# A pooled-attention and softmax-linear feed-forward kernel: first product from pairs of float16 numbers, scaled by powers of two, and one square moved to ScalarE

## The chip, the core and the metric

One Trainium2 chip, one core of it. The time is device time of the launch in microseconds (us). The core's engines are TensorE (PE in the rows, with its weight loads as PEld), VectorE (DVE), ScalarE (ACT), GpSimd (POOL) and SyncE (SP, which here only issues transfers). Each engine takes its instructions in program order and waits on semaphores of the others.

## What is computed

Attention over keys pooled 4x4, followed by a feed-forward block whose middle is h times softmax(h), normalised. The input tensors are float32, apart from w_in and w_out, whose scaling makes them float64.

```python
# attention, per batch of 4: 12288 queries, 768 pooled keys, C = 128
kv_flat = kv.reshape(B, H//4, 4, W//4, 4, C).mean(axis=(2, 4)).reshape(B, -1, C) @ w_sr
k = v = kv_flat
a = softmax((q @ k.T) / sqrt(C))
x = (a @ v).reshape(B * 12288, 128)
# feed-forward, d_ff = 1024
h = x @ w_in                      # the "first product" of the title
e = exp(h - h.max(-1)); sm = e / e.sum(-1)
solu = h * sm
ln = (solu - solu.mean(-1)) / sqrt(solu.var(-1) + 1e-6) * g_ln
out = ln @ w_out
```

## The kernel before, in words

Tokens go in 384 tiles of 128 (4 batches of 96 tiles); four tiles are a group (96 groups). A tile passes a chain of steps, and a loop over 399 slots takes one step of each of several tiles per slot: in slot t the scores of tile t (and the matmuls of tile t+1), and ten slots later (LH) the hidden layer of that tile, thirteen slots later (LO) its last product. From slot 9 (FILL) to six slots past the last tile the order written in the loop is the order on every engine (`manual_schedule`); before and after, a scheduler orders the work.

Precision comes from pairs: a number is a high part plus a low part, and a product is three matmuls (high with high, high with low, low with high). The scores (`scores_pe`, L359) and the first product (`hidden_pe`, L455) use pairs in a float32 format that the PE takes in one pass (f32r; the page of the profile shows it as f32). The other two, attention times values (`values`, L412) and the last product (`final_pe`, L540), use pairs of float16. Per tile that is 6 matmuls of 384 columns, 4.5 of 512 (18 for each group), 6 of 512 and 24 of 128.

What a group of four tiles does once, at slots counted within the group:

- `values_out` on ACT: two scaled copies of the attention output out of PSUM, the high part `xh` (L421) and a full float32 copy `xf` (L422).
- `values_split` on POOL: the low part `xl = xf - xh` (L428). `values_norm` on POOL: `zz` (L435).
- `final_scale` on POOL: four instructions on 4 columns, `f = (z2 + 1e-9) * bound` (L553), `f2 = f * f` (L556), plus `v3` (L557), and the power -1/2 (L558). In the POOL queue they stand ahead of the splits of that slot.
- `q_split` on ACT (L337) and `q_low` on POOL (L345), `rz` on DVE and ACT (L440, L441), the output `ob` on DVE (L564).

What each tile does on POOL: `hidden_split`, the high part of u (L507) and the low part (L508). On ACT: the exponent of the scores (L376), its scaled copy (L378), the square with a sum for the variance (L521), the exponent of h (L476). On DVE: maximum of the scores (L375), u (L490), maximum of h (L461) and its product with 1/z (L467), the low half of the probabilities (L386).

For the next batch, `PLAN` gives slots of the running batch: loads, then 30 additions on POOL (`kv_add`, L201, every second slot from 9 to 67), and from slot 41 on the steps that make keys, values, the norm (`kv_norm_pe`, `kv_norm_out`, `kv_norm_max`) and the bound (`kv_bound`, DVE and POOL, parts at slots 103 and 104, that is 7 and 8 of the batch that uses it). The first batch does the same in `kv_now` and `fill`. The last batch makes nothing for a next one.

At the start w_in is turned from float64 words into a float32 part `wf` and a rest `wr` (`float64_parts`), ACT makes `w_in_h` (L617) and the squares (L619), the PE and DVE the largest column norm `wmax2` (L624), and POOL makes `w_in_l` (L642, L645).

Of the kernel before, what the change touches and what calls it, by code (L numbers as in the profile page):

```python
# [21 lines left out]
P = 128  # L22
# [30 lines left out]
def kernel(  # L53
# [32 lines left out]
    def pow2_under(dst):  # L86

        nc.vector.tensor_single_scalar(
            dst.bitcast(I32), dst.bitcast(I32), 0x7F800000, op=ALU.bitwise_and
        )  # L90
# [33 lines left out]
    def kv_alloc(b):  # L124
        for n, w, dt, bufs in (
            ("kT", NK, F32, 1),
            ("ks", NK, F32, 1),
            ("kh", NK, F32R, 2),
            ("kl", NK, F32R, 2),
            ("ksq", NK, BF16, 1),  # L130
            ("kss", 2, F32, 1),
            ("knm", 2, F32, 1),
            ("vf", NK, F32, 1),
            ("sv", 2, F32, 2),
            ("bb", 2, F32, 2),
        ):
            state[n, b] = bat.tile([P, w], dt, tag=n, name=f"{n}_{b}", bufs=bufs)
        for n in ("vh", "vl"):
            state[n, b] = bat.tile([P, NKC, P], F16, tag=n, name=f"{n}_{b}")
# [125 lines left out]
    def kv_bound(b, part):  # L265

        knm, bb = state["knm", b], state["bb", b]
        if part == 0:
            nc.vector.tensor_tensor(bb[:, 0:1], knm[:, 0:1], knm[:, 1:2], op=ALU.max)
            nc.vector.tensor_scalar(  # L270
                bb[:, 0:1], bb[:, 0:1], wmax2, 1e-20, op0=ALU.mult, op1=ALU.max
            )
            nc.gpsimd.tensor_tensor(bb[:, 0:1], bb[:, 0:1], mhalf[:, 0:1], op=ALU.pow)
        else:
            nc.vector.tensor_scalar(
                bb[:, 1:2], bb[:, 0:1], SC * 1e-3 * 2.0**15, None, op0=ALU.mult
            )
            nc.vector.tensor_scalar(bb[:, 0:1], bb[:, 0:1], SC, None, op0=ALU.mult)

    def kv_vs(b, half):  # L280
# [135 lines left out]
    def values_out(g):  # L416
        b = g * GT // TPB
        xa, sv = state.pop(("xa", g)), state["sv", b][:, 1:2]
        xf = grp.tile([P, 512], F32, tag="xf", name=f"xf_{g}", bufs=1)
        xh = grp.tile([P, 512], F32R, tag="xh", name=f"xh_{g}")  # L420
        nc.scalar.activation(xh, xa, AF.Copy, scale=sv)  # L421
        nc.scalar.activation(xf, xa, AF.Copy, scale=sv)  # L422
        state["xf", g] = (xf, xh)

    def values_split(g):
        xf, xh = state.pop(("xf", g))
        xl = grp.tile([P, 512], F32R, tag="xl", name=f"xl_{g}")
        nc.gpsimd.tensor_tensor(xl, xf, xh.bitcast(F32), op=ALU.subtract)  # L428
        state["x", g] = (xh, xl)

    def values_norm(g):
        b = g * GT // TPB
        zz = grp.tile([P, GT], F32, tag="zz", name=f"zz_{g}", bufs=2)
        rz = grp.tile([P, 2, GT], F32, tag="rz", name=f"rz_{g}", bufs=3)
        nc.gpsimd.tensor_scalar(zz, state.pop(("z", g)), 1e-9, 1.0, op0=ALU.add, op1=ALU.mult)  # L435
        state["zz", g] = (zz, rz)
# [111 lines left out]
    def final_scale(g):  # L548
# [3 lines left out]
        f2 = grp.tile([P, GT], F32, tag="f2", name=f"f2_{g}")  # L552
        nc.gpsimd.tensor_scalar(  # L553
            f, state.pop(("z2", g)), 1e-9, state["bb", b][:, 1:2], op0=ALU.add, op1=ALU.mult
        )
        nc.gpsimd.tensor_tensor(f2, f, f, op=ALU.mult)  # L556
        nc.gpsimd.tensor_tensor(f, f2, state.pop(("v3", g)), op=ALU.add)  # L557
# [27 lines left out]
    w_sr16 = const.tile([P, P], F32, name="w_sr16")  # L585
    w_in_h = const.tile([P, DFF], F32R, name="w_in_h")
    w_in_l = const.tile([P, DFF], F32R, name="w_in_l")
    wch = const.tile([P, NFC, P], F16, name="wch")
    wcl = const.tile([P, NFC, P], F16, name="wcl")
    sw = const.tile([P, 1], F32, name="sw")  # L590
    swi = const.tile([P, 1], F32, name="swi")
    wmax2 = const.tile([P, 1], F32, name="wmax2")

    wsr = const.tile([P, P], F32, name="wsr")
# [21 lines left out]
    wf, wr = float64_parts(raw_in, "in")  # L616
    nc.scalar.copy(w_in_h, wf)  # L617
    wsq = wrk.tile([P, DFF], BF16, tag="junk", name="wsq", bufs=1)
    nc.scalar.activation(wsq, wf, AF.Square)  # L619
    pn = ps_r.tile([P, DFF], F32, tag="r", name="pn")  # L620
    for half in range(2):
        hs = slice(half * 512, half * 512 + 512)
        nc.tensor.matmul(pn[:, hs], ones16, wsq[:, hs], start=True, stop=True)
    nc.vector.tensor_reduce(wmax2, pn, axis=AX.X, op=ALU.max)  # L624

    def kv_now(b, *fs):
# [14 lines left out]
    def w_in_rest():  # L641
        nc.gpsimd.tensor_tensor(wf, wf, w_in_h.bitcast(F32), op=ALU.subtract)  # L642

# [45 lines left out]
    def kv_norms(half):  # L689
# [11 lines left out]
        7: [w_square, partial(kv_bound, 0, 0)],  # L701
        8: [w_norm, partial(kv_bound, 0, 1)],
        9: [w_pow],
# [14 lines left out]
        (77, 0, kv_scale_v), (78, 1, kv_scale_v), (79, 2, kv_scale_v),  # L718
        (79, 0, kv_vs), (81, 1, kv_vs),
        (85, 0, kv_v_pe, kv_norm_out), (87, 0, kv_v_high), (88, 0, kv_v_low),  # L720
        (89, 1, kv_v_pe, kv_norm_out), (91, 1, kv_v_high), (92, 1, kv_v_low),
        (93, 0, kv_norm_pe, kv_norm_out), (96, 0, kv_norm_max),
        (97, 1, kv_norm_pe, kv_norm_out), (99, 1, kv_norm_max),
        (103, 0, kv_bound), (104, 1, kv_bound),
    ]
# [107 lines left out]
```

## Time and profile before

| | us |
|---|---|
| median of three runs | 1951.87 (1951.87 to 1959.1) |
| the profiled execution, its own time | 1954.76 |
| its span, first to last instruction | 1953.0 |
| PE busy, weight loads busy | 1899.8 (97%), 1487.8 (76%) |
| DVE, ACT, POOL busy | 1797.4 (92%), 1783.9 (91%), 1760.0 (90%) |
| granted PE clock, mean | 0.995 of full speed |

All four engines are busy nine tenths of the span or more, so shares of the span don't say which of them sets the pace. A matmul's end in the trace is modelled, and consecutive ones overlap in it: what a matmul costs is read from the distance between starts. Gaps under 0.15 us are an engine's own and are not shown as idle, so POOL's real load is read from its starts as well.

### The profile page before, as it was taken

Reading aid. Unit: us, or ns where it says so; the run is one execution under the profiler, and the core shown is the slowest. Engines: PE = TensorE matmul, PEld = TensorE weight load, DVE = VectorE, ACT = ScalarE, POOL = GpSimd, SP = SyncE. Lnnn points to the kernel's source line nnn. Section 1 sums busy time; section 2 is a strip of 40 time slices with the busy share of each in tenths; the row PEclk is TensorE's granted clock in tenths of the full one; section 3 lists DMA queues with packets and bytes.
Section 4 is the critical chain, followed back from the end, with each engine's and each line's share of the span. In section 5 each row is a group of like instructions: output and inputs, shape, how many; then the busy total and the mean of one; then the engine's idle time right before and its main releaser. Section 6 shows DMA issues by size and latency. Waiting matters only on the chain. (4 is left out here: it accounts for less than half of the span.)

```text
span 1953.0 us, 43521 instructions
## 1 busy us (share of the span) xinstructions
PE 1899.8 (97%) x15678; PEld 1487.8 (76%) x15678; DVE 1797.4 (92%) x2573; ACT 1783.9 (91%) x3141; POOL 1760.0 (90%) x1579
## 2 busy tenths in 40 slices
PE   7999999999999999999999999999999999999997
PEld 4677777777777777777777777777777887787775
DVE  7899999999999999999999999899999999999985
ACT  3998999999999999999999999999999999999995
POOL 3699999999899999999989999999988898988886
PEclk8999999999999999999999999999999999999998
DMA  6899999999999999999999999999999999999996
GB/s 237 174 237 233 235 225 238 221 221 217 213 242 231 238 228 226 226 223 222 217 221 237 237 235 229 228 229 219 223 210 215 223 218 221 225 215 219 224 198 135
DMA packets 1484311, 432.88 MB, mean 222 GB/s; under 512 B 1405889, under 2 KB 1471553, under 8 KB 1483841
## 3 DMA queue, kind: packets, MB, share of 16 engines
q1 hardware_dynamic: 1469840, 410.10, 104.6%
q10 hardware_dynamic: 14256, 20.00, 3.9%
q8 instruction: 125, 2.05, 0.5%
q14 instruction: 90, 0.73, 0.1%
HBM read 52.50 MB, written 25.17 MB: 40 GB/s over the span
## 5 line engine op out<-in xcount | busy, mean ns | idle before, releaser
L508 POOL TENSOR_TENSOR uhl<-u,uhl 128x1024 f16<-128x1024 f32 x384 | 823.2, 2144 | 37.4 <-ACT uhl L505 6.0
L540 PEld LDWEIGHTS <-uT 128*128 128x128 f16 x9216 | 517.5, 98 | 112.8 <-issue 104.6
L540 PE MATMUL o<-wch,uT 128*128 128x128 f16 x6144 | 582.9, 220 | 7.2 <-DMA uT<-uhl 6.8
L540 PE MATMUL o<-wcl,uT 128*128 128x128 f16 x3072 | 536.0, 219 | 0.0
L490 DVE SCALAR_TENSOR_TENSOR u<-h,rz,e 128x1024 f32<-128x1024 f32 x384 | 490.2, 1277 | 24.9 <-ACT e L476 24.5
L461 DVE TENSOR_REDUCE nm<-h 128x1 f32<-128x1024 f32 x384 | 468.9, 1221 | 19.0 <-PE h L455 11.7
L476 ACT ACTIVATE e<-h,nm,rz 128x1024 f32<-128x1024 f32 x384 | 460.1, 1198 | 3.6 <-DVE rz L440 2.8
L521 ACT ACTIVATE junk<-u,su 128x1024 bf16<-128x1024 f32 x384 | 438.0, 1141 | 1.9 <-DVE u L490 1.9
L507 POOL TENSOR_SCALAR uhl<-u 128x1024 f16<-128x1024 f32 x378 | 395.9, 1047 | 10.4 <-DVE u L490 10.2
L412 PE MATMUL xa<-pT,vh 128*128 128x512 f16 x1152 | 391.5, 382 | 7.4 <-DMA pT<-phl 5.2
L375 DVE TENSOR_REDUCE nm<-s 128x1 f32<-128x768 f32 x384 | 365.3, 951 | 34.6 <-PE s L359 34.0
L376 ACT ACTIVATE s<-s,nm 128x768 f32<-128x768 f32 x384 | 335.7, 874 | 60.9 <-DVE nm L375 60.0
L386 DVE SCALAR_TENSOR_TENSOR phl<-s,phl 128x768 f16<-128x768 f32 x384 | 364.9, 951 | 20.0 <-ACT phl L378 10.5
L378 ACT ACTIVATE phl<-s 128x768 f16<-128x768 f32 x384 | 311.4, 811 | 12.0
L455 PE MATMUL h<-w_in_h,xh 128*128 128x512 f32 x768 | 304.9, 478 | 7.0 <-DVE phl L386 3.2
L359 PE MATMUL s<-kh,qh 128*128 128x384 f32 x768 | 264.4, 425 | 7.2 <-DVE u L490 2.8
L455 PE MATMUL h<-w_in_h,xl 128*128 128x512 f32 x768 | 245.1, 400 | 12.0 <-POOL xl L428 11.6
L455 PE MATMUL h<-w_in_l,xh 128*128 128x512 f32 x768 | 240.3, 394 | 0.0
L412 PE MATMUL xa<-pT,vl 128*128 128x512 f16 x576 | 219.1, 380 | 0.0
L359 PE MATMUL s<-kh,ql 128*128 128x384 f32 x768 | 196.2, 337 | 0.0
L359 PE MATMUL s<-kl,qh 128*128 128x384 f32 x768 | 196.1, 336 | 0.0
L455 PEld LDWEIGHTS h<-w_in_h,xh 128*128 128x128 f32 x768 | 140.4, 190 | 72.6 <-issue 18.2
(119 smaller groups left out, 2223.0 us busy)
## 6 DMA issues: line engine op xcount, KB each, us to landing
qf<-in_q_dram SPq DMA_DIRECT2D x96, 256.0 KB, 3.3
out_dram<-ob SPq DMA_DIRECT2D x96, 256.0 KB, 2.8
kv<-in_kv_dram ACTq DMA_DIRECT2D x96, 192.0 KB, 3.1
kv<-in_kv_dram SPq DMA_DIRECT2D x16, 384.0 KB, 7.8
pT<-phl SPq DMA_TRANSPOSE x384, 4.0
uT<-uhl SPq DMA_TRANSPOSE x384, 4.3
raw_in<-in_moe_w_in_dram ACTq DMA_DIRECT2D x1, 1024.0 KB, 6.5
raw_out<-in_moe_w_out_dram SPq DMA_DIRECT2D x1, 1024.0 KB, 7.6
```

The lines of the kernel that those rows point to most:

```text
L359: nc.tensor.matmul(s[:, half, :384], lh[:, ts], rh[:, half * 384 : (half + 1) * 384], start=n == 0, stop=n == 2,)
L375: nc.vector.tensor_reduce(nm, s, axis=AX.XY, op=ALU.max, negate=True)
L386: nc.vector.scalar_tensor_tensor(phl[:, 1], state.pop(("s", t)), SC, phl[:, 0], op0=ALU.mult, op1=ALU.subtract)
L412: nc.tensor.matmul(xa, v[:, c, :], pT[:, :, a * NKC + c, :], start=n == 0, stop=n == len(seq) - 1)
L455: nc.tensor.matmul(h[:, hs], lh[:, ts], rh[:, hs], start=n == 0, stop=n == 2)
L461: nc.vector.tensor_reduce(nm[:, 0:1], state["h", t], axis=AX.X, op=ALU.max, negate=True)
L476: nc.scalar.activation(e, state["h", t], AF.Exp, bias=nm[:, 1:2], scale=state["rz", g][0][:, js], accum_out=state["z2", g][:, js],)
L490: nc.vector.scalar_tensor_tensor(u, state.pop(("h", t)), state["rz", g][1][:, j : j + 1], state.pop(("e", t)), op0=ALU.mult, op1=ALU.mult, ...
L507: nc.gpsimd.tensor_scalar(uhl[:, 0, :], u, 1.0, 1.0, op0=ALU.mult, op1=ALU.mult)
L508: nc.gpsimd.tensor_tensor(uhl[:, 1, :], u, uhl[:, 0, :], op=ALU.subtract)
L521: nc.scalar.activation(junk, u, AF.Square, scale=-float(DFF), bias=su, accum_out=state["v3", g][:, j : j + 1],)
L540: nc.tensor.matmul(po[:, ts], uT[:, a * NFC + c, :], w[:, c, :], start=c == 0 and n == 0, stop=c == NFC - 1 and n == 2,)
```

## The change

x and w_in are split into pairs of float16 in place of f32r, for which both are first scaled by powers of two: w_in by `wsc`, from its largest column norm, and x by a factor from the largest key norm that is multiplied into the scale `sv` of `values_out`. The product of both factors, `bb[:, 3:4]`, is divided out again in `values_norm`, whose second factor was the constant 1.0. The two ACT copies and POOL's subtraction in `values_out` and `values_split` stay and write float16.

In `final_scale` the first two POOL instructions become one ACT instruction, Square with scale and bias from two columns. The loop's order puts it on ACT behind the scaled copy of the scores (L378) and ahead of the square of u (L521) of the same slot.

`kv_bound` gets three parts, at slots 88 to 90 of the batch before, and the norm's steps move ahead of the values' steps, from slots 93 to 99 to slots 77 to 84. At the start, `w_in_h` waits for the norm, and two scalings of 128x1024 are added on ACT.

```diff
-            ("bb", 2, F32, 2),
+            ("bb", 4, F32, 2),
...
+        knm, bb, sv = state["knm", b], state["bb", b], state["sv", b]
         if part == 0:
-            nc.vector.tensor_tensor(bb[:, 0:1], knm[:, 0:1], knm[:, 1:2], op=ALU.max)
+            nc.vector.tensor_tensor(knm[:, 0:1], knm[:, 0:1], knm[:, 1:2], op=ALU.max)
             nc.vector.tensor_scalar(
-                bb[:, 0:1], bb[:, 0:1], wmax2, 1e-20, op0=ALU.mult, op1=ALU.max
+                bb[:, 0:1], knm[:, 0:1], wmax2, 1e-20, op0=ALU.mult, op1=ALU.max
             )
+            nc.vector.tensor_scalar(knm[:, 0:1], knm[:, 0:1], 1e-28, None, op0=ALU.max)
             nc.gpsimd.tensor_tensor(bb[:, 0:1], bb[:, 0:1], mhalf[:, 0:1], op=ALU.pow)
-        else:
+            nc.gpsimd.tensor_tensor(knm[:, 0:1], knm[:, 0:1], mhalf[:, 0:1], op=ALU.pow)
+        elif part == 1:
             nc.vector.tensor_scalar(
                 bb[:, 1:2], bb[:, 0:1], SC * 1e-3 * 2.0**15, None, op0=ALU.mult
             )
             nc.vector.tensor_scalar(bb[:, 0:1], bb[:, 0:1], SC, None, op0=ALU.mult)
+            nc.vector.tensor_scalar(bb[:, 2:3], bb[:, 1:2], 1e-9, None, op0=ALU.mult)
+            pow2_under(knm[:, 0:1])
+        else:
+            nc.vector.tensor_scalar(knm[:, 0:1], knm[:, 0:1], 2.0**5, None, op0=ALU.mult)
+            nc.vector.tensor_scalar(bb[:, 3:4], knm[:, 0:1], wsc, None, op0=ALU.mult)
+            nc.vector.tensor_scalar(sv[:, 1:2], sv[:, 1:2], knm[:, 0:1], None, op0=ALU.mult)
...
-        xh = grp.tile([P, 512], F32R, tag="xh", name=f"xh_{g}")
+        xh = grp.tile([P, 512], F16, tag="xh", name=f"xh_{g}")
...
-        xl = grp.tile([P, 512], F32R, tag="xl", name=f"xl_{g}")
-        nc.gpsimd.tensor_tensor(xl, xf, xh.bitcast(F32), op=ALU.subtract)
+        xl = grp.tile([P, 512], F16, tag="xl", name=f"xl_{g}")
+        nc.gpsimd.tensor_tensor(xl, xf, xh, op=ALU.subtract)
...
-        nc.gpsimd.tensor_scalar(zz, state.pop(("z", g)), 1e-9, 1.0, op0=ALU.add, op1=ALU.mult)
+        nc.gpsimd.tensor_scalar(
+            zz, state.pop(("z", g)), 1e-9, state["bb", b][:, 3:4], op0=ALU.add, op1=ALU.mult
+        )
...
-        nc.gpsimd.tensor_scalar(
-            f, state.pop(("z2", g)), 1e-9, state["bb", b][:, 1:2], op0=ALU.add, op1=ALU.mult
-        )
-        nc.gpsimd.tensor_tensor(f2, f, f, op=ALU.mult)
+        bb = state["bb", b]
+        nc.scalar.activation(
+            f2, state.pop(("z2", g)), AF.Square, scale=bb[:, 1:2], bias=bb[:, 2:3]
+        )
         nc.gpsimd.tensor_tensor(f, f2, state.pop(("v3", g)), op=ALU.add)
...
-    w_in_h = const.tile([P, DFF], F32R, name="w_in_h")
-    w_in_l = const.tile([P, DFF], F32R, name="w_in_l")
+    w_in_h = const.tile([P, DFF], F16, name="w_in_h")
+    w_in_l = const.tile([P, DFF], F16, name="w_in_l")
...
     wf, wr = float64_parts(raw_in, "in")
-    nc.scalar.copy(w_in_h, wf)
...
     nc.vector.tensor_reduce(wmax2, pn, axis=AX.X, op=ALU.max)
+    nc.vector.tensor_scalar(wsc, wmax2, 1e-28, None, op0=ALU.max)
+    nc.gpsimd.tensor_tensor(wsc, wsc, mhalf[:, 0:1], op=ALU.pow)
+    pow2_under(wsc)
+    nc.vector.tensor_scalar(wsc, wsc, 2.0**14, None, op0=ALU.mult)
+    nc.scalar.mul(wf, wf, wsc)
+    nc.scalar.copy(w_in_h, wf)
+    nc.scalar.mul(wr, wr, wsc)
...
-        8: [w_norm, partial(kv_bound, 0, 1)],
+        8: [w_norm, partial(kv_bound, 0, 1), partial(kv_bound, 0, 2)],
...
+        (77, 0, kv_norm_pe, kv_norm_out), (80, 0, kv_norm_max),
+        (81, 1, kv_norm_pe, kv_norm_out), (84, 1, kv_norm_max),
         (85, 0, kv_v_pe, kv_norm_out), (87, 0, kv_v_high), (88, 0, kv_v_low),
+        (88, 0, kv_bound), (89, 1, kv_bound), (90, 2, kv_bound),
         (89, 1, kv_v_pe, kv_norm_out), (91, 1, kv_v_high), (92, 1, kv_v_low),
-        (93, 0, kv_norm_pe, kv_norm_out), (96, 0, kv_norm_max),
-        (97, 1, kv_norm_pe, kv_norm_out), (99, 1, kv_norm_max),
-        (103, 0, kv_bound), (104, 1, kv_bound),
```

## Rows read from the trace of the kernel before

**Rows 1.** busy by stretch: length, then busy of PE, PEld, DVE, ACT, POOL

```profile
131.00:350.00 219.00, 213.17 (x1784) 167.66 (x1784) 201.55 (x287) 202.05 (x357) 209.73 (x188) 1.00 1.15 232
...
1297.00:1893.00 596.00, 593.22 (x4993) 470.21 (x4992) 565.17 (x813) 563.57 (x995) 534.24 (x474) 1.00 1.10 218
```

**Rows 2.** busy time by stretch, of line L376 alone: two instructions a tile

```profile
131.00:350.00 219.00, 43.38 (x89) 1.00 1.15 232
```

**Rows 3.** timeline of POOL, one group at 300 us: start, duration, instruction

```profile
299.63 1.29 POOL L428 TENSOR_TENSOR xl<-xf,xh 128x512 fp32r<-128x512 f32 x1
...
309.73 0.27 POOL L553 TENSOR_SCALAR f<-z,bb 128x4 f32<-128x4 f32 x1
...
310.36 0.20 POOL L557 TENSOR_TENSOR f<-f,v 128x4 f32<-128x4 f32 x1
...
319.49 1.28 POOL L428 TENSOR_TENSOR xl<-xf,xh 128x512 fp32r<-128x512 f32 x1
```

**Rows 4.** timeline of PE, one group after 1297 us

```profile
1592.02 0.38 PE L412 MATMUL xa<-pT,vl 128*128 128x512 f16 x1
...
1593.72 0.38 PE L412 MATMUL xa<-pT,vl 128*128 128x512 f16 x1
1593.75 0.81 PE L455 MATMUL h<-w_in_h,xh 128*128 128x512 f32 x2
...
1595.33 0.23 PE L540 MATMUL o<-wch,uT 128*128 128x128 f16 x1
...
1611.13 0.38 PE L412 MATMUL xa<-pT,vl 128*128 128x512 f16 x1
```

**Rows 5.** timeline of PE, a run of float16 matmuls of 512 columns

```profile
55.67 0.59 PE L412 MATMUL xa<-pT,vh 128*128 128x512 f16 x2
...
58.05 0.38 PE L412 MATMUL xa<-pT,vl 128*128 128x512 f16 x1
```

**Rows 6.** instructions by line and form: busy, mean ns | idle before

```profile
L508 POOL TENSOR_TENSOR uhl<-u,uhl 128x1024 f16<-128x1024 f32 x384 | 823.2, 2144 | 37.4 <-ACT uhl L505 6.0
...
L428 POOL TENSOR_TENSOR xl<-xf,xh 128x512 fp32r<-128x512 f32 x96 | 122.8, 1279 | 41.8 <-ACT xf L422 37.0
...
L441 ACT ACTIVATE rz<-rz,bb 128x4 f32<-128x4 f32 x96 | 28.1, 293 | 2.6 <-DVE rz L440 2.6
L553 POOL TENSOR_SCALAR f<-z,bb 128x4 f32<-128x4 f32 x96 | 25.9, 270 | 10.7 <-ACT e L476 0.9
...
L435 POOL TENSOR_SCALAR zz<-z 128x4 f32<-128x4 f32 x96 | 18.7, 194 | 7.9
...
L305 POOL TENSOR_TENSOR vl<-vf,vh 128x384 f16<-128x384 f32 x8 | 7.4, 925 | 0.2
...
L275 DVE TENSOR_SCALAR bb<-bb 128x1 f32<-128x1 f32 x4 | 0.6, 147 | 0.7 <-POOL bb L273 0.7
```

**Rows 7.** timeline of POOL and ACT around 1600 us, idle time in brackets

```profile
1595.49 1.27 POOL L428 TENSOR_TENSOR xl<-xf,xh 128x512 fp32r<-128x512 f32 x1 [1.09 <-ACT xf L422]
...
1604.84 0.27 POOL L553 TENSOR_SCALAR f<-z,bb 128x4 f32<-128x4 f32 x1
...
1605.82 1.14 ACT L521 ACTIVATE junk<-u,su 128x1024 bf16<-128x1024 f32 x1
```

**Rows 8.** timeline of ACT beside the POOL group of rows 3

```profile
306.65 0.81 ACT L378 ACTIVATE phl<-s 128x768 f16<-128x768 f32 x1
```

**Rows 9.** timeline of ACT, two exponents of the scores four tiles apart

```profile
523.67 0.88 ACT L376 ACTIVATE s<-s,nm 128x768 f32<-128x768 f32 x1 [1.71 <-DVE nm L375]
...
542.23 0.87 ACT L376 ACTIVATE s<-s,nm 128x768 f32<-128x768 f32 x1
```

**Rows 10.** timeline of DVE, PE and ACT at the start

```profile
34.00 1.22 DVE L624 TENSOR_REDUCE wmax<-pn 128x1 f32<-128x1024 f32 x1
...
62.06 0.74 PE L455 MATMUL h<-w_in_h,xh 128*128 128x512 f32 x2 [0.87 <-DVE sw L88]
...
58.96 0.71 ACT L421 ACTIVATE xh<-xa,sv 128x512 fp32r<-128x512 f32 x1
```

More of the change, by code (lines that the diff above doesn't have):

```diff
@@ L265, in kv_bound @@
     def kv_bound(b, part):
-        knm, bb = state["knm", b], state["bb", b]
+        knm, bb, sv = state["knm", b], state["bb", b], state["sv", b]
         if part == 0:
-            nc.vector.tensor_tensor(bb[:, 0:1], knm[:, 0:1], knm[:, 1:2], op=ALU.max)
+            nc.vector.tensor_tensor(knm[:, 0:1], knm[:, 0:1], knm[:, 1:2], op=ALU.max)
             nc.vector.tensor_scalar(
-                bb[:, 0:1], bb[:, 0:1], wmax2, 1e-20, op0=ALU.mult, op1=ALU.max
+                bb[:, 0:1], knm[:, 0:1], wmax2, 1e-20, op0=ALU.mult, op1=ALU.max
             )
+            nc.vector.tensor_scalar(knm[:, 0:1], knm[:, 0:1], 1e-28, None, op0=ALU.max)
             nc.gpsimd.tensor_tensor(bb[:, 0:1], bb[:, 0:1], mhalf[:, 0:1], op=ALU.pow)
-        else:
+            nc.gpsimd.tensor_tensor(knm[:, 0:1], knm[:, 0:1], mhalf[:, 0:1], op=ALU.pow)
+        elif part == 1:
             nc.vector.tensor_scalar(
@@ L592 @@
     wmax2 = const.tile([P, 1], F32, name="wmax2")
+    wsc = const.tile([P, 1], F32, name="wsc")
     wsr = const.tile([P, P], F32, name="wsr")
@@ L641, in w_in_rest @@
     def w_in_rest():
-        nc.gpsimd.tensor_tensor(wf, wf, w_in_h.bitcast(F32), op=ALU.subtract)
+        nc.gpsimd.tensor_tensor(wf, wf, w_in_h, op=ALU.subtract)
     def w_in_low():
```

## The prediction

> **What bounds the kernel now.** The shares of the whole span say nothing, since four engines stand between 90 and 97%. I read the busy time by stretch first. From 1297 to 1893 us, in the last batch, the PE is busy for 593.2 of 596 us and POOL for 534.2; from 131 to 350 us POOL has 209.7 of 219 and the PE falls back to 213.2 [rows 1]. So there are two kinds of stretch, with different bounds.
>
> The timelines confirm it. In the late stretch one group of four tiles takes the PE from 1592.02 to 1611.13 us, 19.11 us or 4.78 a tile [rows 4], and inside it POOL stands idle, 1.09 us ahead of `xl` alone [rows 7]. There the PE sets the pace. Around 300 us POOL goes from one `xl` to the next in 19.86 us, 4.965 a tile, with no idle time shown in these rows or between them [rows 3]. That group holds two additions for the next batch's keys (L201), which the late group lacks. There POOL sets the pace, and the PE waits a little. The stretch from 131 to 350 us has 89 instructions of a line that has two a tile [rows 2], so 44.5 tiles at 4.92 us. By the plan of the additions there are three such stretches: 133 tiles. Of the 384 tiles I leave 12 to the start (the first hidden layer comes in slot 10); 239 are left for the PE-bound kind.
>
> **PE: float16 for the first product.** Between the last `xa` matmul at 1593.72 and the first of the last product at 1595.33 lie seven steps (start of `xa`, six of h): 1.61 us [rows 4]. What a float16 matmul of the same 512 columns costs is in the same trace: eleven steps from 55.67 to 58.05 us, 0.216 each [rows 5]. Seven of them are 1.515. The change saves 0.095 us a tile, 0.38 a group: 19.11 becomes 18.73, 4.68 a tile. The number of matmuls and columns is unchanged, so this is all that the PE gets.
>
> **POOL: two instructions less a group, and a cheaper subtraction.** From the start of L553 to the start of L557 are 0.63 us [rows 3]; both instructions in it go. For `xl` in float16 the trace has no row. It is bounded from above by its present 1.28 us (nothing gained) and from below by the two subtractions that mix float32 with float16: 925 ns for 384 columns, 2144 for 1024, a line that gives 1.17 us at 512 [rows 6]. I take that, since the types are the same as in those rows: 0.11 saved. `zz` reads its second factor from a column, as L553 does, which takes 270 ns where `zz` has 194: 0.08 more [rows 6]. Together 0.66 us a group: 19.86 becomes 19.20, 4.80 a tile.
>
> On `xl` the Trainium skill (GPSIMD Engine Reference, Instruction dispatch) speaks against the gain: a two-input operation there can take in one operand per cycle, with a floor of about 2.5 cycles an element, and no type is named. The rows differ by type: 2144 ns for 1024 is 2.1 ns an element with a float16 operand, 1279 for 512 is 2.5 ns without [rows 6]. By the page's rule the group would save 0.55 and not 0.66, some 4 us less over the three stretches.
>
> **ACT: the square.** 96 instructions on 4 columns. The nearest row is L441, 293 ns with one factor from a column [rows 6]; a second column could make it somewhat longer, and neighbours overlap. Between 0.2 and 0.4 us a group, I take 0.3. In the late group it lands at 1605.82, where L521 begins now [rows 7]. ACT is busy for 563.6 of 596 us [rows 1], or 18.1 of the group's 19.1; with the square 18.4, under 18.73. That ACT and DVE together can go faster than the PE does today is seen after a stall: two exponents four tiles apart start 18.56 us from each other [rows 9]. So the PE stays the bound of the late kind, with 1% to spare.
>
> **The new wait.** POOL's addition (L557) now waits for ACT's square, and behind it in POOL's queue stand the power and the splits of that tile, and behind those the transposes on SP and the last product. In the late group POOL comes to this place at 1604.84, and the square can't end before 1605.82 + 0.29 = 1606.11 [rows 6, 7]: a wait of 1.27 us where 0.63 of work went, so POOL is 0.64 us later. It has 1.09 idle ahead of the next `xl` [rows 7], which covers it; of that 0.38 goes as the group shortens, and 0.07 or so is left, or a delay as small. Without this cover a group costs up to 0.64 more. In the POOL-bound group the copy that the square follows ends at 306.65 + 0.81 = 307.46, and POOL comes at 309.73 [rows 3, 8], over two microseconds after: no wait there.
>
> **What follows for the stretches.** In the 239 tiles of the PE-bound kind 0.095 each: 22.7 us. In the 133 others between 0.165 each, if POOL is late from the first tile on (21.9), and 4.92 - 4.68 = 0.24 each, if POOL never becomes the bound again (31.9). POOL's deficit shrinks from 4.965 - 4.78 = 0.19 to 0.12 a tile, so it takes half as long again to run out of lead; I take a quarter of the stretch at 0.24 and the rest at 0.165: 24.4. Together 47.1.
>
> **Start and bounds.** The largest norm is there at 34.00 + 1.22 us, the first h begins at 62.06 [rows 10]. Behind the norm come four small instructions on DVE and POOL (I allow 2 us), three on ACT of the size of L521, 1.14 each [rows 7], one of which was there before, and POOL's two of the size of L508, 2.14 each [rows 6], so the w_in pair is there by about 46 and h doesn't wait. But 2.3 us of ACT come into a stretch in which ACT feeds the first scores, and the first `xh` at 58.96 [rows 10] must now have the bound first, which before it didn't need. Between 0 (all in gaps) and 6; I take 3. In each of three batches `kv_bound` has six more DVE instructions, at 147 ns [rows 6] 0.9 us, and one more power on POOL, for which DVE waits at the front of a slot; from 0 to 4 us a batch, if a split of POOL lies ahead, I take 0.5: 1.5 in all. The norm's steps that move are as many as before and each takes the place of one that was moved away: 0.
>
> **The sum.** 47.1 - 3 - 1.5 = 42.6 us. The profiled execution took 1954.76 (span 1953.0), 2.9 more than the median of three, 1951.87; from the profiled time it gives 1912.2, from the median 1909.3. I give 1910.
>
> **Rivals.**
> - ACT and DVE take over before the PE's gain is paid. For it: ACT, DVE and the PE hand work to each other in every slot, and ACT's 18.4 is close to 18.73. Against: 18.56 was run [rows 9]. If the late group stays at 19.11, only the 24.4 remain: 1952 - 24.4 + 4.5 = 1932.
> - POOL doesn't get its gain, since the square arrives late or `xl` costs what it did. Then the 133 tiles gain little, and 22.7 - 4.5 is left: 1934.
> - The transposes set the pace: the chip moves 218 to 232 GB/s in both kinds of stretch (the last column of [rows 1]), and a faster slot asks for more. Against: the PE shows no wait for them in the late group. If they did, the time would stay: 1950.
> - Slower: the wait for the square in every group. If ACT falls behind POOL, so that the square ends 1.3 us or more after POOL comes to it in the POOL-bound stretches too, and one ACT instruction later (1.0) than figured, POOL loses 2.3 - 0.63 = 1.6 us in each of 96 groups where it is or becomes the bound: in 33 groups of the first kind 1.6 - 0.03, and in 60 of the late kind, beyond the cover of 1.09, 0.5. That is 52 + 30 + 4.5: 2038. It decides from 0.63 us of wait in rows 3's place on; the rows show POOL two microseconds behind ACT there, so it needs ACT to lose its lead.
>
> **How the numbers follow.** Forecast 0.75; ACT and DVE 0.09; POOL without gain 0.07; transposes 0.04; slower 0.05. The forecast's own bounds: all at their best, 31.9 + 22.7 with nothing at the start, 1952 - 54.6 = 1897; with 6 at the start, 4 a batch, and the page's floor, 1952 - 47 + 18 + 4 = 1927. To hold 8 in 10 the range takes in the two rivals at 1932 and 1934: 1897 to 1934. A measurement of this kernel tells about 0.5% from no change, that is 9.8 us: faster than 1942 has 0.90, the same 0.05, slower 0.05.
>
> **What would show it.** In the profile after: the seven steps around h at 1.51 us, weight loads of h as short as the last product's; POOL's group around 300 us at 19.2 with L557 directly behind a split, or shorter by the stretch's gain; in the late stretch POOL idle ahead of L557, released by ACT, and still some idle ahead of `xl`; a late group of 18.7 us on the PE with the PE busy nearly throughout. Wrong would be: DVE or ACT busy throughout with the PE waiting for them in the late stretch, PE waits for `xl` or for transposes that weren't there, or a first `xh` that is later by more than 6 us.

## The result and the profile after

| | before | after |
|---|---|---|
| median, us | 1952.65 (1951.87 to 1959.1) | 1929.45 (1927.93 to 1935.31) |
| ratio to before | | 0.988 [0.9849, 0.991] |
| span of the profiled execution | 1953.0 | 1926.1 |

The change is worth 23 us by the medians and 26.9 by the two profiled spans, of the 42.6 that the sum gave. Most of the parts that were worked out are there; something that the sum doesn't hold takes most of the rest back.

The page of the changed kernel (busy time, share and instructions; then groups with busy time, mean ns of one | idle time just before):

```profile
PE 1855.6 (96%) x15677; PEld 1308.1 (68%) x15678; DVE 1795.2 (93%) x2600; ACT 1803.2 (94%) x3239; POOL 1705.3 (89%) x1392
...
L553 PEld LDWEIGHTS <-uT 128*128 128x128 f16 x9216 | 546.6, 98 | 109.1 <-DMA uT<-uhl 21.6
L553 PE MATMUL o<-wch,uT 128*128 128x128 f16 x6144 | 578.6, 220 | 14.9 <-DMA uT<-uhl 13.4
...
L468 PEld LDWEIGHTS <-xh 128*128 128x128 f16 x1536 | 145.1, 98 | 205.7 <-DVE phl L397 41.9
...
L468 PE MATMUL h<-w_in_h,xl 128*128 128x512 f16 x768 | 230.0, 381 | 1.0 <-POOL xl L439 0.6
```

The PE is still at 96%, now with less to do: it is busy for 44 us less (1899.8 before), and the span is only 27 us shorter. Lines have moved by up to 13: h is L468 (L455 before), the last product L553 (L540), `xl` L439 (L428), the splits of u L520 and L521 (L507, L508). The weight loads of h take 98 ns like those of the last product. The matmuls of o are held up 13.4 us by `uT`, the transpose of u that SP issues. Before had 6.8 of these, all behind 1900 us; now 5.7 lie ahead of 1850 us (table below).

The two instructions moved off POOL are one on ACT (the view of instructions by line):

```profile
L439 POOL TENSOR_TENSOR xl<-xf,xh 128x512 f16<-128x512 f32 x96 | 111.3, 1159 | 13.2 <-ACT xf L433 6.5
...
L567 ACT ACTIVATE f<-z,bb 128x4 f32<-128x4 f32 x96 | 36.4, 379 | 0.0
...
L570 POOL TENSOR_TENSOR f<-f,v 128x4 f32<-128x4 f32 x96 | 19.3, 201 | 85.7 <-ACT f L567 85.1
```

POOL now waits 85 us in all for the square, at L570 (L557 before). The PE's timeline shows the first product: the last `xa` matmul's successors begin at 656.19, 656.62, 657.05, and the last product at 657.48, so two steps in 0.43 us, where the 1.61 for seven steps of [rows 4] is 0.46 for two.

```profile
656.19 0.60 PE L468 MATMUL h<-w_in_h,xh 128*128 128x512 f16 x2
656.62 0.60 PE L468 MATMUL h<-w_in_l,xh 128*128 128x512 f16 x2
657.05 0.60 PE L468 MATMUL h<-w_in_h,xl 128*128 128x512 f16 x2
657.48 0.22 PE L553 MATMUL o<-wch,uT 128*128 128x128 f16 x1
```

Where the gain is and where it is not follows from the starts of the 384 exponents of the scores (one a tile), summed by kind of stretch. The additions and loads for the next batch's keys lie at tiles 12 to 76 of each of the first three batches ("load stretches"), the steps that the plan moves at tiles 76 to 108. The forecast's column is the prediction's sum put into the same classes: 24.4 for 133 tiles, 0.095 for each of the other 59 of the load stretches, and so on.

| us | before | after | gain | forecast |
|---|---|---|---|---|
| start, to tile 12 | 74.1 | 73.3 | 0.7 | -3 |
| load stretches, 192 tiles | 950.0 | 934.0 | 16.0 | 30.0 |
| tiles 76 to 108 of three batches | 470.1 | 466.0 | 4.1 | 7.6 |
| tiles 300 to 383 | 398.6 | 391.0 | 7.7 | 7.9 |
| from the last exponent on | 60.2 | 61.7 | -1.5 | 0.1 |

### The profile page after: what moved, and what is told of

Read it like the earlier page. It is cut to its first block, busy times and chain, and to the rows that moved or that the text cites. A ratio compares the mean times of both kernels' runs of the same rounds, so it can differ in the third digit from the quotient of the medians.

```text
span 1926.1 us, 43006 instructions
## 1 busy us (share of the span) xinstructions
PE 1855.6 (96%) x15677; PEld 1308.1 (68%) x15678; DVE 1795.2 (93%) x2600; ACT 1803.2 (94%) x3239; POOL 1705.3 (89%) x1392
## 5 line engine op out<-in xcount | busy, mean ns | idle before, releaser
L521 POOL TENSOR_TENSOR uhl<-u,uhl 128x1024 f16<-128x1024 f32 x384 | 819.5, 2134 | 38.2 <-ACT uhl L518 6.7
L553 PEld LDWEIGHTS <-uT 128*128 128x128 f16 x9216 | 546.6, 98 | 109.1 <-DMA uT<-uhl 21.6
L553 PE MATMUL o<-wch,uT 128*128 128x128 f16 x6144 | 578.6, 220 | 14.9 <-DMA uT<-uhl 13.4
L553 PE MATMUL o<-wcl,uT 128*128 128x128 f16 x3072 | 535.7, 220 | 0.0
L474 DVE TENSOR_REDUCE nm<-h 128x1 f32<-128x1024 f32 x384 | 468.7, 1221 | 10.9 <-PE h L468 10.5
L520 POOL TENSOR_SCALAR uhl<-u 128x1024 f16<-128x1024 f32 x378 | 394.7, 1044 | 7.2 <-DVE u L503 7.0
L468 PEld LDWEIGHTS <-xh 128*128 128x128 f16 x1536 | 145.1, 98 | 205.7 <-DVE phl L397 41.9
L468 PE MATMUL h<-w_in_h,xh 128*128 128x512 f16 x768 | 231.0, 383 | 13.7 <-DVE phl L397 7.3
L468 PE MATMUL h<-w_in_h,xl 128*128 128x512 f16 x768 | 230.0, 381 | 1.0 <-POOL xl L439 0.6
L468 PE MATMUL h<-w_in_l,xh 128*128 128x512 f16 x768 | 230.5, 382 | 0.0
```

Source lines behind the costliest of these rows:

```text
L468: nc.tensor.matmul(h[:, hs], lh[:, ts], rh[:, hs], start=n == 0, stop=n == 2)
L474: nc.vector.tensor_reduce(nm[:, 0:1], state["h", t], axis=AX.X, op=ALU.max, negate=True)
L520: nc.gpsimd.tensor_scalar(uhl[:, 0, :], u, 1.0, 1.0, op0=ALU.mult, op1=ALU.mult)
L521: nc.gpsimd.tensor_tensor(uhl[:, 1, :], u, uhl[:, 0, :], op=ALU.subtract)
L553: nc.tensor.matmul(po[:, ts], uT[:, a * NFC + c, :], w[:, c, :], start=c == 0 and n == 0, stop=c == NFC - 1 and n == 2,)
```

## The experiments

Theory: the parts cost what was worked out, and the missing 20 us come from the transfers. A faster slot brings the loads of keys (ACT's queue) and the transposes (SP's queue) closer together, a transpose lands later, and the PE, which now has less cover, waits for it. Rivals: the wait for the square; the plan's moved steps; SP's queue, in which a late transpose of u holds up the transpose of p behind it; ACT's time for issuing the loads. The runs follow in three groups. A span, and everything read from a trace, is of the run's profiled execution. "Late stretch" is tiles 300 to 348, in which nothing is done for a next batch. Line numbers in short diffs are left out.

### The square and its wait

**e1: the changed kernel, with the two instructions back on POOL.**

```diff
-        nc.scalar.activation(f2, state.pop(("z2", g)), AF.Square, scale=bb[:, 1:2], bias=bb[:, 2:3])
+        nc.gpsimd.tensor_scalar(f, state.pop(("z2", g)), 1e-9, bb[:, 1:2], op0=ALU.add, op1=ALU.mult)
+        nc.gpsimd.tensor_tensor(f2, f, f, op=ALU.mult)
```

> The changed kernel with one part undone: the two instructions of final_scale are on POOL again, the float16 pair, its scaling and the plan stay. Late transposes (theory: what is missing was lost where the next batch's keys are loaded, since transposes land later there and the PE waits for them): POOL's group in those stretches grows from 18.96 us to 19.6, 0.16 a tile over 133 tiles, some 20 us slower, less what fewer late transposes give back: 1938 to 1950, and the late stretch stays at 4.66 a tile. Wait for the square (rival: POOL stands idle 85 us ahead of the addition, and what it hands on is late): the wait is gone, no slower than the changed kernel, 1915 to 1930.

1935.34 us (1933.45 to 1938.65), ratio 0.9906 [0.9892, 0.9919], span 1933.7: between the two expectations. So the square on ACT is worth some 6 us within the change, though the two intervals overlap: 10.5 in the load stretches (944.6 against 934.0), of which 5.3 are lost at tiles 76 to 108 (460.7 against 466.0). The late stretch is the same, 4.677 us a tile in both. The wait for the square doesn't make the kernel slower; that rival falls.

**e2: the kernel before, with the square on ACT alone** (first product in f32r, as before).

```diff
-        nc.gpsimd.tensor_scalar(f, state.pop(("z2", g)), 1e-9, state["bb", b][:, 1:2], op0=ALU.add, op1=ALU.mult)
-        nc.gpsimd.tensor_tensor(f2, f, f, op=ALU.mult)
+        nc.scalar.activation(f2, state.pop(("z2", g)), AF.Square, scale=bb[:, 1:2], bias=bb[:, 2:3])
...
+            nc.vector.tensor_scalar(bb[:, 2:3], bb[:, 1:2], 1e-9, None, op0=ALU.mult)
```

> The kernel before with one part of the change alone: the square on ACT, first product in f32r as before. Late transposes: the PE-bound tiles stay at 4.78 us, POOL's group in the load stretches goes from 19.86 to 19.2 us, 0.16 a tile over 133 tiles, about 20 us less: 1930 to 1936. Wait for the square: POOL's saving is taken back by its waiting, 1948 to 1956.

1937.41 us (1932.11 to 1949.99), ratio 0.9918 [0.9895, 0.9942], span 1948.0. By the median a little short of what was expected. The late stretch stays at 4.786 us a tile, the value before: there the square brings nothing and the float16 product all. With the square on ACT, waits of the PE ahead of `xa` rise here too: gaps between starts of matmuls, as far as they are 0.6 us or more over the matmul's own step, sum to 11.7 us ahead of `xa` and 3.1 ahead of o, where before has 7.4 and 0. (The profiled execution is the slowest of the six here, 12 us above their median.)

**e4: the square one slot earlier on ACT**, so that POOL doesn't wait for it.

```diff
-    def final_scale(g):
+    def final_square(g):
...
+    def final_scale(g):
...
+        at_last(slot - FSC + 1, final_square)
```

> The changed kernel with the square given to ACT one slot earlier, so that POOL's addition finds it done. Wait for the square: most of the 85 us of POOL's idle time ahead of the addition goes, splits and transposes leave earlier, 1910 to 1922. Late transposes: the idle time moves to another place in POOL (ahead of xl, for ACT's copy), the PE's pace stays at 4.66 in the late stretch, and the time stays within 4 us: 1925 to 1932.

1929.57 us (1922 to 1938.57), ratio 0.9877 [0.9854, 0.99], span 1933.2: no difference. The wait at `f` is gone, and POOL waits elsewhere (the same view, of e4):

```profile
L439 POOL TENSOR_TENSOR xl<-xf,xh 128x512 f16<-128x512 f32 x96 | 111.2, 1158 | 41.9 <-ACT xf L433 39.0
...
L573 POOL TENSOR_TENSOR f<-f,v 128x4 f32<-128x4 f32 x96 | 19.3, 201 | 0.0
```

85 us of one wait against 32.5 more of another, and no gain from it: POOL's idle time in the PE-bound stretches is slack, as the prediction had it. The late stretch is slightly longer, 4.718 us a tile.

### The transfers

**e5: the kernel before, without the 96 loads of the next batches' keys.** Left out is part of the computation: the keys and values of batches 2 to 4 come from a constant tile.

```diff
-        nc.scalar.dma_start(
-            state["kv", b, half, r][:, two, :], kv[b - 1, r, :, k0 : k0 + 384]
-        )
+        state["kv", b, half, pos // 2] = state["kv_once"]
```

> The kernel before without the loads of the keys of batches 2 to 4 (96 transfers of 192 KB): the additions on POOL stay and read one tile that is set once, so that part of the computation is left out. Late transposes: POOL still sets the pace in the stretches with additions; the PE waited there 7.4 us for transposes of the probabilities, so 3 to 8 us less than before: 1944 to 1949. Rival: transfers cost nothing before either, 1952.

1954.1 us (1953.06 to 1956.15), ratio 0.9999 [0.999, 1.0008], span 1952.7. I had expected a gain; there is none. In the kernel before the loads cost nothing.

**e6: the changed kernel with the same edit** (the same part of the computation left out).

> The changed kernel without the same loads. Late transposes: the PE's 16 us of waiting for the probabilities and 6 for u go, and with them three stretches at the lower clock, 12 to 22 us less than the changed kernel: 1907 to 1917, and the distance to the kernel before without loads grows from 23 to 30 us or more. Rival (wait for the square, or ACT and DVE): the waits stay and so does the distance: 1922 to 1929.

1909.26 us (1907.64 to 1910.94), ratio 0.9772 [0.9756, 0.9789], span 1905.8. The same loads cost the changed kernel 20 us, and without them it stands where the forecast had it. Busy time in one load stretch (length, then busy of PE, PEld, DVE, ACT, POOL with their instructions, granted clock, share of the DMA engines, GB/s), of before, after, e6 and then e12 (below):

```profile
599.00:815.00 216.00, 210.69 (x1753) 164.93 (x1751) 198.21 (x282) 199.45 (x352) 206.69 (x187) 1.00 1.15 233
```

```profile
599.00:815.00 216.00, 207.59 (x1759) 146.50 (x1757) 198.32 (x283) 201.58 (x363) 200.31 (x166) 0.98 1.19 234
```

```profile
599.00:815.00 216.00, 212.60 (x1840) 151.59 (x1839) 205.70 (x293) 209.77 (x378) 209.16 (x172) 1.00 1.10 222
```

```profile
599.00:815.00 216.00, 212.29 (x1828) 151.51 (x1827) 205.96 (x295) 209.03 (x377) 207.95 (x172) 1.00 1.17 241
```

In the same 216 us the PE of after gets through 1759 matmuls, hardly more than the 1753 of before; without the loads it is 1840, at fewer GB/s. By stretches e6 has 914.6 us in the load stretches (after 934.0) and 466.3, 391.2 and 60.3 in the last three rows of the table: all that the loads cost is in the stretches where they run, and in the profiled tail.

**e10: the loads stay in ACT's queue, but bring 16 of 384 columns** into a tile that nobody reads (the same part left out as in e5).

```diff
-        nc.scalar.dma_start(
-            state["kv", b, half, r][:, two, :], kv[b - 1, r, :, k0 : k0 + 384]
-        )
+        scrap = dmt.tile([P, 16], F32, tag="scrap", name=f"scrap_{b}_{part}", bufs=9)
+        nc.scalar.dma_start(scrap, kv[b - 1, r, :, k0 : k0 + 16])
```

> The changed kernel in which each of the 96 loads of later keys is still issued by ACT but brings 16 columns in place of 384 into a tile that nobody reads; the additions read one tile that is set once, so the later keys are left out of the computation. If the bytes of the loads cost what was gained by leaving them out (20 us): as without loads, 1906 to 1913. If ACT's time to issue them did: as the changed kernel, 1925 to 1932.

1909.55 us (1907.29 to 1912.27), ratio 0.9768 [0.9753, 0.9783], span 1908.2. As fast as without any: it is the bytes of the loads, not the time in which ACT issues them.

**e11: each load as two halves of 64 partitions, one slot apart** (with the plan of e3, below).

```diff
-            state["kv", b, half, r][:, two, :], kv[b - 1, r, :, k0 : k0 + 384]
+            state["kv", b, half, r][0:64, two, :], kv[b - 1, r, 0:64, k0 : k0 + 384]
+    def kv_load_rest(b, part):
...
+            state["kv", b, half, r][64:128, two, :], kv[b - 1, r, 64:128, k0 : k0 + 384]
...
+    PLAN += [(5 + 2 * r - 2 * (r // RR), r, kv_load_rest) for r in range(2 * RR)]
```

> The changed kernel with the plan of e3 and each load of later keys given in two halves of 64 partitions, one slot apart: the same bytes in bursts half as long. If a load hurts as a burst that stands in front of a transpose: transposes land earlier, 1908 to 1919. If the bytes themselves hurt, since the engines of the transfers have hardly a gap at this pace: as e3, 1921 to 1928.

1920.98 us (1918.93 to 1922.16), ratio 0.9829 [0.9815, 0.9842], span 1917.1: between the two expectations. It gains some 4 us on e3's median, and the intervals of the two overlap slightly.

### Queues and the plan

**e3: the changed kernel with the plan's norm and bound steps back in their late slots.**

```diff
-        (77, 0, kv_norm_pe, kv_norm_out), (80, 0, kv_norm_max),
-        (81, 1, kv_norm_pe, kv_norm_out), (84, 1, kv_norm_max),
...
-        (88, 0, kv_bound), (89, 1, kv_bound), (90, 2, kv_bound),
...
+        (93, 0, kv_norm_pe, kv_norm_out), (96, 0, kv_norm_max),
+        (97, 1, kv_norm_pe, kv_norm_out), (99, 1, kv_norm_max),
+        (100, 0, kv_bound), (101, 1, kv_bound), (102, 2, kv_bound),
```

> The changed kernel with the norm's steps at slots 93 to 99 again, as before the change, and the three parts of the bound at slots 100 to 102. If the plan's move costs what the two traces show between slots 72 and 108 of a batch (a gain of 1.5 us where 3.4 to 4 were due, and 5.1 us more than a quiet stretch between 76 and 88): 2 to 2.5 us a batch less, 1920 to 1924. If those stretches are only the same work at another place: 1928 to 1931.

1924.54 us (1921.4 to 1930.8), ratio 0.9853 [0.9836, 0.987], span 1923.0: 5 us under the change by the medians, with overlapping intervals.

**e12: e3 with the loads issued by SP**, in whose queue the transposes stand.

```diff
-        nc.scalar.dma_start(
+        nc.sync.dma_start(
```

> The changed kernel with the plan of e3 and the loads of later keys issued by SP, in one queue with the transposes, so that a load's bytes don't run beside a transpose that was issued before it. If it is the running side by side that hurts: 1908 to 1919. If the bytes themselves hurt: as e3, 1921 to 1928, or more, as SP has 0.4 us more to issue in every second slot, up to 1935.

1914.73 us (1910.99 to 1919.22), ratio 0.9802 [0.9784, 0.9819], span 1912.9. It leaves nothing of the computation out, and is 15 us faster than the change.

**e13: the same single edit on the changed kernel, with its own plan.**

> The changed kernel with one edit: the loads of the next batch's keys are issued by SP, in whose queue the transposes stand, instead of ACT. The plan of the norm and of the bound stays the change's own. Theory one (the queue alone is the cause, the plan is worth little): 1913 to 1920, within 5 us of the same edit with the plan put back (1914.73), and the stretches at tiles 76 to 108 add up to 155, as in the changed kernel. Theory two (the plan was half of that gain): 1920 to 1926, near the plan put back alone (1924.5). Theory three (with SP's loads the plan's move is even a gain): under 1911.

1921.84 us (1916.92 to 1925.06), ratio 0.9834 [0.9815, 0.9852], span 1914.8: theory two by its number. (The profiled execution is the fastest of the four.) With it the four corners of a square are there:

| median, us (ratio) | plan of the change | plan put back |
|---|---|---|
| loads issued by ACT | 1929.45 (0.988) | 1924.54 (0.9853) |
| loads issued by SP | 1921.84 (0.9834) | 1914.73 (0.9802) |

The other queue brings 8 to 10 us, the late plan 5 to 7, and the two add up. The differences down the columns are better secured than those along the rows: 0.9802 and 0.9853 have separate intervals, the others touch. The traces place only a part of the plan's 5 to 7: 1.7 at tiles 76 to 108 (466.1 in e13 against 464.4 in e12) and 1.3 at tiles 348 to 383 (166.5 against 165.2).

**e7 and e8: the transpose of u one slot later in SP's queue, in the changed kernel and in the kernel before.**

```diff
-LO = 13
+LO = 14
...
-        uhl = dmt.tile([P, 2, DFF], F16, tag="uhl", name=f"uhl_{t}", bufs=3)
+        uhl = dmt.tile([P, 2, DFF], F16, tag="uhl", name=f"uhl_{t}", bufs=4)
...
-        at(i - 1, hidden_turn)
+        at(i - 2, hidden_turn)
```

> The changed kernel with u's transpose given to SP one slot later and the last product one slot later (LO 14), with a fourth buffer for u's halves. In the load stretches of the changed kernel the probabilities' transpose stood 2.5 us in SP's queue on average after its data were there, behind u's transpose, which waits for POOL. Theory (SP's queue passes POOL's lateness on to the probabilities): that wait goes below 1 us, the PE's waits for the probabilities go, and the time is 8 to 18 us below the changed kernel, 1911 to 1921. Rival (the transfers' own length under load alone): the wait in the queue goes, the PE's waits stay, 1926 to 1933.

1935.18 us (1926.12 to 1938.95), ratio 0.9894 [0.9874, 0.9914], span 1930.4: above both expectations.

> The kernel before with the same move of u's transpose alone. POOL sets the pace in its load stretches whenever the probabilities come, so by both theories little: 1946 to 1954.

1956.81 us (1955.59 to 1958.26), ratio 1.0009 [1.0001, 1.0018], span 1954.6. That is slightly over what was expected. Neither run gains time, but neither excludes SP's queue as a cause. In e7 the edit does a part of what it was made for: in the load stretches the issue row of the transpose of p ends 3.13 us in the mean after VectorE finishes the probabilities, for 4.18 in the change, and the gaps ahead of `xa` sum to 7.7 us, for 16.2 (in e8 to none, for 7.4). It also costs elsewhere: the gaps ahead of the scores grow from 3.2 to 6.7 us, those of h ahead of `xh` from 0.6 to 4.1, and the late stretch, where no loads run, takes 4.744 us a tile for 4.677. Over 192 tiles that would be 13 us, an estimate, which could hide a gain.

### What a late transpose does

The trace of the changed kernel shows one case whole. First the PE's matmuls and its weight loads (idle time ahead of a row in brackets, with what ended it), then the end of the probabilities on DVE, SP's and ACT's issues, and busy time in the stretch behind it (columns as under e6):

```profile
663.32 0.22 PE L553 MATMUL o<-wch,uT 128*128 128x128 f16 x1
666.41 0.39 PE L423 MATMUL xa<-pT,vh 128*128 128x512 f16 x1 [2.88 <-ACT rz L454]
...
667.77 0.65 PE L423 MATMUL xa<-pT,vh 128*128 128x512 f16 x1
668.21 0.63 PE L423 MATMUL xa<-pT,vl 128*128 128x512 f16 x1
668.64 0.64 PE L423 MATMUL xa<-pT,vh 128*128 128x512 f16 x1
```

```profile
666.41 0.10 PEld L423 LDWEIGHTS <-vh 128*128 128x128 f16 x1 [3.05 <-DMA pT<-phl]
```

```profile
654.30 0.95 DVE L397 SCALAR_TENSOR_TENSOR phl<-s,phl 128x768 f16<-128x768 f32 x1
```

```profile
651.74 5.94 SPq L400 DMA_TRANSPOSE pT<-phl  x1
657.79 2.00 SPq L526 DMA_TRANSPOSE uT<-uhl  x1
659.84 0.57 SPq L339 DMA_DIRECT2D qf<-in_q_dram  x1
660.50 1.28 SPq L400 DMA_TRANSPOSE pT<-phl  x1
661.95 4.20 SPq L526 DMA_TRANSPOSE uT<-uhl  x1
```

```profile
660.95 0.40 ACTq L186 DMA_DIRECT2D kv<-in_kv_dram  x1
```

```profile
667.50:671.00 3.50, 3.50 (x11) 1.27 (x10) 2.16 (x3) 1.97 (x4) 2.91 (x3) 0.51 1.16 262
671.00:700.00 29.00, 29.00 (x251) 20.68 (x250) 26.83 (x37) 26.18 (x47) 23.87 (x21) 1.00 1.17 236
```

The probabilities are finished at 655.25 (counted in order, the 132nd `phl` belongs to the 132nd transpose of p). SP comes to their transpose 5.25 us later, at 660.50, behind the transpose before it, one of u and a load of queries (`qf`). ACT issues a load of keys at 660.95. The transpose lands 5.9 us after the start of its issue, at 666.4, where the median of that stretch is 4.6, and the PE, done with o at 663.5, stands for 2.88 us. So it is late by two things, its place in SP's queue and a slow landing. The row of the matmul names `rz`, which it doesn't read; the weight load beside it names `pT`, and that is the one. Behind the stop the granted clock is 0.51 in the row at 667.50, the lower of the two levels (1.2 GHz), and matmuls of 512 columns start 0.43 us apart instead of 0.22; in the next row it is back at 2.4. So this stop costs part of its length again. In the profiled run of the change the clock falls three times between 50 and 1850 us (near 180, 667 and 767 us, behind stops of 2.0, 2.9 and 2.4 us), in e7 three times, in e3 twice, in e4 and e10 once, in before, e6, e11, e12 and e13 not once. Not every such stop is followed by a fall: before has one of 2.20 us at 159.5 us, e1 one of 3.07 at 668.8 and e3 one of 3.04 at 1031.4, each with the clock at 1.00 behind it. Half the speed for three stretches like the one at 667.50 is an estimate of 5 us of the 20.

How long a transpose takes from the end of its issue row to its landing, from 75 us on: median, the value that 9 in 10 stay under, and the longest, apart for those beside which a load of keys was in flight and the others. Behind them the PE's gaps as counted under e2 (75 to 1850 us):

| | `uT` beside a load, us | `uT` without | `pT` beside a load | `pT` without | gaps ahead of `xa` | of o | of h for `xl` |
|---|---|---|---|---|---|---|---|
| before | 2.59, 3.78, 4.5 | 2.08, 2.68, 4.3 | 2.54, 4.07, 4.9 | 2.20, 3.62, 4.6 | 7.4 | 0 | 11.3 |
| after | 2.67, 4.21, 7.3 | 2.10, 3.40, 4.7 | 2.63, 3.83, 5.2 | 2.23, 3.64, 4.6 | 16.2 | 5.7 | 0 |
| e6, no loads | none | 2.10, 3.04, 4.8 | none | 2.23, 3.67, 4.8 | 6.3 | 0 | 2.0 |
| e13, loads on SP | 2.10, 3.38, 4.3 | 2.10, 3.33, 4.6 | 2.31, 3.90, 4.5 | 2.20, 3.49, 4.6 | 14.7 | 1.4 | 0 |

Beside a load from ACT's queue a transpose takes 0.3 to 0.6 us more in the median, in before as in after, and the longest of `uT` 2.6 more in after (7.3 for 4.7). Beside one from SP's queue `uT` takes no more and `pT` 0.1. Before has the delay too, but no gap ahead of o; after has 5.7 us of them, and twice the gaps ahead of `xa`. In e13 the gaps ahead of o are nearly gone and those ahead of `xa` stay.

The gaps and the clock account for the loads' cost: 21.9 us of gaps in after less 8.3 in e6 is 13.6, with the 5 of the clock 18.6, and the load stretches of after are 19.5 us longer than those of e6. Between e13 and e6 the load stretches differ by 7.3 us (921.9 against 914.6), about what the gaps ahead of `xa` do (14.7 against 6.3).

The trace also says at which transpose these gaps arise. A group's four transposes of p fill one tile, which `xa` reads whole, so only the last of the four can hold it up; and SP issues that one right behind a load of queries (256 KB) in nearly every group. All gaps ahead of `xa` in the table (6, 10, 7 and 12 of them) lie there. In e6, where no load of keys runs, a transpose of p right behind a load of queries takes 2.70 us to land in the median and any other 2.12. For this last transpose the loads of keys don't lengthen the landing in the mean (load stretches: 3.00 us in after, 3.19 in e6), but it leaves SP's queue later: its issue row ends 4.23 us after its data in after, 3.59 in e6. In the ten gaps of after both are long, 4.4 to 6.5 and 2.9 to 5.2 us. How much of a gap is queue and how much is landing no run here separates, and none moves the load of queries.

## Why the prediction was right or wrong

**Right by its range, with a term missing.** 1929.45 lies between 1897 and 1934, 19 us above the 1910 named. That it lies inside is luck: the forecast's own bounds end at 1927, the range reached to 1934 for the sake of two rivals, and neither of them came true. One of the prediction's own signs of being wrong is there too, PE waits for transposes that weren't there. The total of the sum was good to a few us for a kernel without the loads (e6 has 1909.26), though several of its terms were off and cancel.

**PE, float16: right, slightly small.** The late stretch goes from 4.786 to 4.677 us a tile, 0.109 less against 0.095 by [rows 4, 5]; the 48 tiles without a transfer for the next batch give 18.71 us a group, where 18.73 was forecast. e2, without the float16 product, leaves it at 4.786.

**POOL: right, the saving too small.** The group around 300 us, from `xl` to `xl`, is 18.98 us (forecast 19.20, before 19.86 in [rows 3]), and POOL is packed throughout:

```profile
294.93 1.17 POOL L439 TENSOR_TENSOR xl<-xf,xh 128x512 f16<-128x512 f32 x1
...
304.72 0.20 POOL L570 TENSOR_TENSOR f<-f,v 128x4 f32<-128x4 f32 x1
305.00 1.02 POOL L571 TENSOR_TENSOR f<-f,mhalf 128x4 f32<-128x4 f32 x1
...
313.91 1.16 POOL L439 TENSOR_TENSOR xl<-xf,xh 128x512 f16<-128x512 f32 x1
```

L570 has no wait here, as said. `xl` takes 1159 ns in the mean where the line through two other shapes gave 1.17 us. The Trainium skill (GPSIMD Engine Reference, Instruction dispatch) gives a two-input floor of about 2.5 cycles an element and names no type. The prediction read the cycles as ns and the floor as a price, and so had `xl` stay at 1.28 by that rule; a floor in cycles doesn't say that, and 1159 ns for 512 elements (2.26 ns each) doesn't contradict it. What the rows do show is that the type counts. In e6 the load stretches take 914.6 us, 35.4 less than before. POOL still sets the pace there, with 2.4 us of idle time in all three: its group is 0.88 us shorter, where 0.66 was forecast, and 0.22 a tile for 133 tiles with 5.6 for the rest make 34.9. A quarter at the PE's pace isn't needed for it.

**The new wait: right.** In the late group POOL waits for the square and has none left ahead of `xl` (timeline of POOL):

```profile
1597.89 2.13 POOL L521 TENSOR_TENSOR uhl<-u,uhl 128x1024 f16<-128x1024 f32 x1
1601.57 0.20 POOL L570 TENSOR_TENSOR f<-f,v 128x4 f32<-128x4 f32 x1 [1.54 <-ACT f L567]
...
1609.44 0.27 POOL L446 TENSOR_SCALAR zz<-z,bb 128x4 f32<-128x4 f32 x1
1609.79 1.16 POOL L439 TENSOR_TENSOR xl<-xf,xh 128x512 f16<-128x512 f32 x1
```

1.54 us against 1.27, and the 1.09 of idle time ahead of `xl` [rows 7] is used up, by that and by the shorter group. The late group runs at its forecast all the same, and e4, which takes the wait away, gains nothing. The rival at 2038 needed ACT to lose its lead in the load stretches. There POOL waits for the square 18.8 us in the change and 2.4 in e6, so mostly where the loads have made the PE stop, and e4, without this wait, is no faster there (934.7 us).

**ACT's square: right in size, wrong as free.** 379 ns in the mean for 0.2 to 0.4. But at tiles 76 to 108, where ACT also has steps for the next batch, it costs time: 3.7 us in e2 (473.8 against 470.1 before), 5.3 in the change (466.0 against 460.7 in e1).

**Start and plan: off, in opposite directions.** The start gains 0.7 us where it was to lose 3. At tiles 76 to 108 the gain is 4.1 for 7.6: 5.0 are lost there, where 1.5 was put down for the bound and 0 for the moved steps. With the square back on POOL (e1) the gain there is 9.4, all that the PE was to bring, with the moved steps and the larger bound in place; with the plan put back (e3) it is 5.7. So the loss comes with the square, and the moved steps add 1.6 to it. In detail tiles 76 to 92 are 2.5 us a batch longer than before (0.7 in e1, 3.0 in e4) and tiles 92 to 108 3.8 shorter. Since e4 has no wait for the square, it isn't POOL's wait that costs this; the work that ACT has gained is what is left, which is argued.

**The step that failed: the transfers at no cost.** The prediction put the loads' and transposes' traffic into a rival of its own ("the transposes set the pace") with one price for the whole kernel, 1950, and a chance of 0.04. It argued against it from the late group, where the PE shows no wait. But in the late group there are no loads; these run in the POOL-bound stretches alone, and there the landing of the transposes beside them was not read. What would have had to be in the sum is a term for those 192 tiles: 19.5 us measured between after and e6, against 14 that are missing from the forecast's 30.0. It couldn't have been read off the trace before as a wait that is there, since in that kernel the loads are covered (e5: nothing gained without them).

Shown are the ends of the chain (loads away: 20 us; their bytes away: the same; another queue: 8 to 10), the gaps and the clock that make up the cost, and one gap in full. Why the same loads cost nothing before is argued: a PE that stands ahead of `xl` anyway (11.3 us of gaps) doesn't wait for a transpose that lands meanwhile, and a faster POOL takes this cover away. e1 bears that out for u alone: with POOL slower again (20.7 us of gaps ahead of `xl`) the gaps ahead of o are gone, but those ahead of `xa` are 14.4, nearly as many as in the change. Whether the loads act through the landing of a transpose or through its place in SP's queue stays open.

## What to carry to other kernels

A transfer that costs nothing in the kernel before may be hidden by the very wait that a change removes. So where a change shortens the slot, price each transfer of that stretch anew: the latest landing there, with its wait in the issuing queue, against the time until its reader comes, not whether a wait shows today; and read it in the stretch where other transfers run beside it. Plain loads that run beside transposes are worth trying in the transposes' own queue: one word in the code brought a third of what the whole change did.

## What the runs showed of the hardware

- **The issuing queue of a load matters beside transposes.** The same bytes issued by SP in place of ACT: 1924.54 becomes 1914.73, 1929.45 becomes 1921.84, and a transpose of u beside a load takes 2.10 us in the median against 2.67. The Trainium skill (DMA: Bandwidth & Descriptors, Issuing engines are not separate DMA queues) says that transfers from all engines end on the same 16 DMA engines, and that issuing from several only saves issue time. By that alone the edit would bring nothing or lose a little; e12 and e13 show 8 to 10 us. The runs don't tell whether it is the one queue or the moment: behind the transposes in SP's queue a load also starts later than ACT would start it. SP's queue by itself is no shelter: behind a load of queries, which SP issues too, a transpose of p takes 2.70 us in the median for 2.12 (e6).
- **Throughput isn't the measure.** e12 moves 241 GB/s in the stretch shown above, after 234, and e12 is the faster one.
- **A stop of the PE can be followed by half the clock.** After a stop of 2.88 us the row at 667.5 has 0.51, and matmuls of 512 columns at 0.43 us. All three falls of the change in mid-run lie behind stops of 2.0 to 2.9 us, but stops of 2.2 us (before) and 3.0 to 3.1 us (e3, e1) had none.
